# An S4 convolution beside a mixture of experts: chunks overlapped, paced by what each slot has left, and the final sums spread over the last block

## The chip, the cores and the metric

The kernel runs on one core of a Trainium2 chip. The metric is the device time of one execution in microseconds (us), as the median of several runs. A profile of one execution shows what each engine did: TensorE (PE, with its weight loads as PEld), VectorE (DVE), ScalarE (ACT), GpSimd (POOL) and SyncE (SP). Each engine takes its instructions in the order of the program and waits where a semaphore is not yet set. SP and POOL are used here to issue DMAs.

## The reference

The input is 2048 tokens of 512 channels. After a layer norm, two branches are added to the input:

```python
x = A_u
xn = _layernorm(x, axis=-1)
return x + _A_ref(xn, ...) + _B_ref(xn, ...)
```

Branch A is an S4 layer: for each of 512 channels a kernel K of length 2048 is made from 128 complex modes (`K = einsum("dn,dnl,dn->dl", Cc, P, dB).real`, with `P = exp(dt*A*l)`), the channel is convolved with it along the tokens, and `xn * Dskip` is added. Branch B is a mixture of 8 experts with top 8 of 8, so every token goes through every expert: `out += w * (silu(xn @ w1[e]) @ w2[e])` with 1792 hidden channels and softmax gates.

## The kernel before, in words

**Blocks and slots.** The experts are the main loop: 8 experts `e`, in each 4 blocks `tb` of 512 tokens, in each block 4 groups `d` of hidden channels (`DQS`: 2, 2, 2 and 1 pairs `pr` of 256), in each group 4 slots `s`. One call of `block(e, tb, d)` (L1116) issues the products with W1 (L1016, seven products in place of eight, in the manner of Strassen), and calls `slot` (L1078) after each quarter of them. Values are kept as a high and a low float16 part, and three matmuls make one product. ACT copies partial sums between PSUM banks for the next product (`hb`, L1142 and L1148), makes the activation (L1032) and its high part (L1034). DVE makes the low part (L1037). Parts of the seven products are combined by adding DMAs on POOL's queue (`add`, L1114: scC<-sE, scB<-sE). The second products, with W2 (L1000 to L1002), are taken from a list `units`, some in each slot, by `pop`. The results are scaled by the gate and added to `oacc` in DRAM by POOL's queue (L980).

**What a slot does** (L1078 to L1094), in this order: it pops units, flushes the low parts of a slot ago, runs what is pinned to this slot (`side`, filled by `put`), makes the low parts of converted weights (`work_lows`), does up to `limit` steps of weight work (`work_on`; three in the first block, two in the first and last block of an expert, else one), and lets the background go on (`bg_run`). Then the slot counter goes up. The order on each engine is the order in which Python issues the instructions, and no scheduler changes it.

**Weight work** (L376 to L510). An `Item` has a load, one to three steps, and a condition. For an expert to come, each pair of W1 and W2 is loaded once and squared on ACT (L379), which gives a scale, and later loaded again and converted. A pair of W1 takes three steps: sums of its parts on DVE into `tw` (L393 to L395), conversion of the raw parts on ACT (L382), conversion of `tw` on ACT. The low parts on DVE (L385) follow in the next slot. There is one `tw` buffer and four raw buffers. `fetch` issues loads on SP as buffers come free. Outside the first block `work_on` looks at the first item of the list alone; in the first block at the first four.

**The background** is one generator: layer norm and transposes of the tokens (`xprep`), then the S4 branch (`s4_all`, L762). It yields the planned DVE time of each piece (by `tt_(n) = n / 960 + 0.14`), or None while it waits for a slot (`hold(stamp)` waits until the slot counter is past the stamp). S4 goes in 32 chunks of 16 channels. A chunk has tables on DVE (`s4_tables`, L612 to L614, six steps), its kernel on PE (`s4_kernel`, L626, and 16 DMAs L637), its input loaded by SP (`s4_uload`, L643) and normalised on DVE (`s4_unorm`, L648, L649), transforms of input and kernel on PE (`s4_uf` L656, `s4_kf` L665), the products and sums in the transformed domain on DVE (`s4_conv`, L675 to L704), and the way back on PE (`s4_back` L713, `s4_out` L719 and a DMA to `ys4` in DRAM). Every second chunk a `s4_basis` is made for two chunks on DVE, with sines on ACT, which `run_later` lets run in slot 2 of d = 1 and d = 2 only. All PE steps of S4 share one PSUM bank; `take_bank` copies the last result out before the next is made.

In `s4_all` before, step c first normalises input c-1, then sends chunk c-2 back, transforms chunk c-1, with the tables of chunk c advanced by one step at each of these places; then the rest of the tables; then, side by side (`together`), the conv of chunk c-1, the kernel of chunk c and at times a basis.

**How much background a slot gets** (`bg_run`, L930). The planner keeps the planned PE time and the planned DVE time in `clock`. Before, the background goes on while the DVE total is under both 0.9 of the PE total and, in this slot, 1.15 of the PE time since the last slot. At the last block `bg_until("s4")` runs what is left of S4 with no other work beside it.

**The end.** `s4_final` (L1096) adds the 16 tiles of `ys4` to `oacc` by DMAs on POOL's queue (L1098) and, for the 12 tiles that are finished then, sends them to the output on SP's queue. It is pinned to one slot: expert 7, last block, d = 1, s = 0. The last four tiles are loaded again (`final_load`) and finished by DVE.

Of the kernel before, what the change touches and what calls it, by code (L numbers as in the profile page):

```python
# [13 lines left out]
ALU = mybir.AluOpType  # L14
# [3 lines left out]
P = 128  # L18
# [14 lines left out]
def s4_moe_kernel(  # L33
# [62 lines left out]

    uts = {}

    clock = {"slot": 0, "pe": 0.0, "pe0": 0.0, "dve": 0.0, "dve0": 0.0}
    bank = {"out": None}  # L100

    def take_bank(out=None):

        f, bank["out"] = bank["out"], None
        if f:
            f()
        bank["out"] = out
# [308 lines left out]

    done = set()
    work = []
    live = {"n": 0}

    def piece_square(e, w, pr, ready):
        return Item(lambda: load_raw(e, w, pr, "pp"), [lambda raw: square(e, w, pr, raw)], ready)
# [37 lines left out]
    def fetch():  # L460

        n = 0
        for it in work:
            if it.load is not None:
                if it.raw is None:
                    if live["n"] >= NRAW:
                        return
                    it.raw = it.load()
                    live["n"] += 1
                n += 1  # L470
                if n >= NRAW:
                    return

    def work_on(limit):
        while limit > 0:
            it = None
            for c in work[:4]:
                if c.ready() and not (c.sums and len(c.steps) == 3 and any(l[2] for l in lows)):
                    it = c
                    break  # L480
                if c.load is None or not early["on"]:
                    break
            if it is None:
                break
            fetch()
            if it.load is not None and it.raw is None:
                break
            low = it.steps.pop(0)(it.raw)
            limit -= 1
            last = not it.steps  # L490
            if last:
                work.remove(it)
            if low:
                lows.append((low, last, it.sums and last))
            elif last and it.load is not None:
                live["n"] -= 1
        fetch()

    early = {"on": True}

    lows = []

    def work_lows():

        while lows:
            low, last, _ = lows.pop(0)
            low()
            if last:
                live["n"] -= 1


    s4 = {}
# [75 lines left out]
    def s4_tables(c):  # L588
        g, h = c // 2, c % 2
        wv, zr, zi = s4["basis", g]  # L590
        tb = sb.tile([P, 2, 3, DC, 32], F32, tag="tb", name=f"tb{c}", bufs=1)
        V.memset(tb[:, 0, 0, :, 0:1], 1.0)
        V.memset(tb[:, 1, 0, :, 0:1], 0.0)
        V.tensor_copy(tb[:, :, 1, :, 0], wv[:, :, h * DC:(h + 1) * DC])
        for st in range(6):
            L = min(1 << st, 32)
            s0, s1, ns = (0, 2, 2) if st < 5 else (1, 2, 1)
            nn = ns * DC
            tin = tb[:, :, s0:s1, :, 0:L].rearrange("p c s d l -> p c (s d) l")
            if st < 5:  # L600
                tout = tb[:, :, 0:2, :, L:2 * L].rearrange("p c s d l -> p c (s d) l")
            else:
                tout = tb[:, :, 2, :, :]
            k0 = 2 * st
            n4 = [P, 2, nn, L]
            zrv = zr[:, h, k0:k0 + ns, :].rearrange("p k d -> p (k d)").unsqueeze(1).unsqueeze(3).to_broadcast(n4)
            ziv = zi[:, :, h, k0:k0 + ns, :].rearrange("p c k d -> p c (k d)").unsqueeze(3).to_broadcast(n4)
            ta = sb.tile([P, 1024], F32, tag="ta", name=f"ta{c}_{st}", bufs=1)[:, :2 * nn * L]
            ta = ta.rearrange("p (c n l) -> p c n l", c=2, n=nn)
            tt = sb.tile([P, 1024], F32, tag="tt", name=f"tt{c}_{st}", bufs=1)[:, :2 * nn * L]  # L610
            tt = tt.rearrange("p (c n l) -> p c n l", c=2, n=nn)
            V.tensor_tensor(ta, tin, zrv, op=ALU.mult)  # L612
            V.tensor_tensor(tt, tin[:, ::-1], ziv, op=ALU.mult)  # L613
            V.tensor_tensor(tout, ta, tt, op=ALU.add)  # L614
            yield 3 * tt_(2 * nn * L) + 0.3 * (st == 0)
        s4["tb", c] = tb

    def s4_kernel(c):
        tb = s4["tb", c]
        take_bank(lambda: s4_kernel_out(c))  # L620
        kg_ = ps_s.tile([P, 4, 64], F32, tag="s4", name=f"kgen{c}")
        for dg in range(4):
            for cc in range(2):
                for dsb in range(4):
                    d = dsb * 4 + dg
                    T.matmul(kg_[32 * dsb:32 * dsb + 32, dg, :], tb[:, cc, 0, d, :],  # L626
                             tb[:, cc, 1:3, d, :], start=(cc == 0), stop=(cc == 1))
        s4["kgen"] = kg_
        clock["pe"] += 1.2
# [94 lines left out]
    def tt_(n):  # L724

        return n / 960 + 0.14

    def hold(stamp):

        while clock["slot"] <= stamp:  # L730
            yield None

    def now():
        return clock["slot"]
# [14 lines left out]
                yield None  # L749
                waits = 0  # L750

    def s4_kgen(c, stamp):
        yield from hold(stamp + 1)
        s4_kernel(c)
        at = now()
        yield 0.0
        yield from hold(at)
        take_bank()
        s4["kt_at"] = now()
        yield 0.0  # L760

    def s4_all():  # L762
        s4_raw(0)
        for _ in s4_dt():
            yield 3.0
        yield 2.2
        yield from s4_basis(0)
        z_at = at = -1
        for c in range(NCH + 2):
            tab = s4_tables(c) if c < NCH else iter(())  # L770

            def step():
                return next(tab, 0.0)
            if 0 < c <= NCH:
                s4_unorm(c - 1)
                un_at = at = now()
                yield 2 * tt_(256) + step()
            else:
                yield step()
            yield step()  # L780
            if c > 1:
                yield from hold(z_at + 1)
                s4_back(c - 2)
                at = now()
                yield step()
                yield from hold(at)
                take_bank()
                at = now()
            else:
                yield step()  # L790
            yield step()
            if 0 < c <= NCH:
                yield from hold(max(at, un_at + 1))
                s4_uf(c - 1)
                at = now()
            yield step()
            if 0 < c <= NCH:
                yield from hold(max(at, s4["kt_at"] + 1))
                s4_kf(c - 1)
                at = now()  # L800
            yield step()
            for cost in tab:
                yield cost
            gens = []
            if 0 < c <= NCH:
                yield from hold(at)
                gens.append(s4_conv(c - 1))
            if c < NCH:
                s4_uload(c)
                gens.append(s4_kgen(c, max(at, now())))  # L810
            if c % 2 and c // 2 + 1 < NCH // 2:
                gens.append(s4_basis(c // 2 + 1))
            yield from together(gens)
            z_at = now()


    load_x(0)
# [103 lines left out]
        done.add("s4")  # L921

    bg = background()
    SHARE = 0.9

    def steps(n):
        for _ in range(n):
# [2 lines left out]
    def bg_run():  # L930


        most = clock["dve0"] + 1.15 * (clock["pe"] - clock["pe0"])
        clock["pe0"] = clock["pe"]
        while "s4" not in done and clock["dve"] < min(most, SHARE * clock["pe"]):
            c = next(bg, None)
            if c is None:
                break
            clock["dve"] += c
        clock["dve0"] = clock["dve"]  # L940

    def bg_until(key):
# [135 lines left out]
    def slot(e, tb, d, s, pops):  # L1078
        if e + tb == 0:
            work_lows()  # L1080
        pop(pops)
        flush()
        if s == 2 and 0 < d < len(DQS) - 1:
            run_later()
        for f in side.get((e, tb, d, s), ()):
            f()
        work_lows()
        early["on"] = e + tb == 0
        work_on(3 if e + tb == 0 else 2 if tb == NB - 1 or tb == 0 else 1)
        if (e, tb, d) >= (0, 2, 1):  # L1090
            if (e, tb, d, s) == (0, 2, 1, 0):
                clock["pe"] = clock["pe0"] = clock["dve"] = clock["dve0"] = 0.0
            bg_run()
        clock["slot"] += 1  # L1094

    def s4_final():  # L1096
        for i in range(NT):
            nc.gpsimd.dma_start(oacc[i], ys4[:, i, :], accum_op=ALU.add)  # L1098
            if i < NT - TPB:
                nc.sync.dma_start(out[i * P:(i + 1) * P, :], oacc[i])  # L1100
        done.add("s4f")

    put((E - 1, NB - 1, 1, 0), s4_final)

    def final_load(j):
        i = NT - TPB + j
# [139 lines left out]
```

## Time and profile before

| | us |
|---|---|
| median of 3 runs | 2522.05 (2519.59 to 2524.8) |
| the profiled execution | 2520.7 |
| its span, first to last instruction | 2518.9 |
| mean granted PE clock, share of full | 0.978 |

The profile's page gives busy time by engine and the span in slices. A table of stretches gives, for each stretch named, its length, the busy time of each engine, the granted clock and the DMA share. A row of the waits names who waited for whom, the total in us, how often, and the longest. A row of a timeline gives start, duration, engine, line, what is written and read, and in brackets how long the engine stood idle before it and what ended that. A row of the chain gives start and duration of the piece of work that the end waited for.

### The profile page before, as it was taken

The page shows a single profiled execution, that of the slowest core. Times are in us where ns is not written, and L with a number is a line of the kernel's source. Part 1 is how long each engine was busy: PE and PEld are TensorE (multiplying, and loading weights), DVE is VectorE, ACT ScalarE, POOL GpSimd, SP SyncE. Part 2 cuts the span into 40 slices and gives each one's busy share as a digit, 9 for nine tenths or more (in the row PEclk, how much of TensorE's full clock was granted, in tenths as well). Part 3 has the DMA queues.
Part 4 walks back from the last instruction along what each step waited for, and adds up shares of the span by engine and source line. Part 5 has one row for each costly group of instructions (what it writes and reads, how often), then busy time and mean ns, then how long its engine had stood idle before and what let it go on. Part 6 is the DMA issues. An engine that isn't in the chain of part 4 may idle for free.

```text
span 2518.9 us, 45497 instructions
## 1 busy us (share of the span) xinstructions
PE 2385.4 (95%) x17749; PEld 1599.0 (63%) x17749; DVE 1935.2 (77%) x3808; ACT 1418.1 (56%) x2394; POOL 346.0 (14%) x402
## 2 busy tenths in 40 slices
PE   5799889998999999999999999999999999899996
PEld 5466556655666666666666666666666666566663
DVE  7534897778879889959999879978998778986411
ACT  5666365553655647455564556665475565554442
POOL 0000001111111110111110111111011111011130
PEclk8899999999999999999999999999999999999998
DMA  7566346755656535555454554654465554434354
GB/s 233 151 159 161 75 114 150 167 110 126 140 130 139 136 75 145 110 125 127 89 151 111 131 112 98 164 130 100 109 141 117 126 136 89 126 55 78 71 124 115
DMA packets 266903, 311.32 MB, mean 124 GB/s; under 512 B 130176, under 2 KB 158848, under 8 KB 266368
## 3 DMA queue, kind: packets, MB, share of 16 engines
q1 hardware_dynamic: 209664, 212.97, 27.9%
q0 software_dynamic: 57024, 95.45, 24.2%
q8 instruction: 139, 2.28, 0.4%
q14 instruction: 76, 0.62, 0.1%
HBM read 196.11 MB, written 56.62 MB: 100 GB/s over the span
## 4 chain that ended last, share of the span: by engine, by line
PE 69%; DVE 13%; issue 7%; DMA 5%; ACT 4%; SPq 2%; POOL 1%; DVEq 0%; POOLq 0%; ACTq 0%
PE hb L1016 31%; PE y L1002 11%; PE y L1000 11%; PE y L1001 11%; DVE ahl L1037 2%; SPq L637 2%; DVE tm L695 2%; DVE w1s L385 2%; DVE s L696 1%; PE kgen L626 1%; DMA oacc<-ys 1%; PE yp L713 1%; PE uf L656 1%; PE kf L665 1%; DMA ut<-in_u_dram 1%
## 5 line engine op out<-in xcount | busy, mean ns | idle before, releaser
L1016 PE MATMUL hb<-xop,w1s 128*128 128x256 f16 x9408 | 1129.2, 276 | 80.1 <-ACT hb L1148 36.0
L1016 PEld LDWEIGHTS <-w1s 128*128 128x128 f16 x9408 | 927.0, 99 | 280.7 <-issue 75.8
L1002 PE MATMUL y<-w2s,ahl 128*128 128x512 f16 x1792 | 680.6, 380 | 8.9 <-DVE ahl L1037 8.9
L1000 PE MATMUL y<-w2s,ahl 128*128 128x512 f16 x1792 | 681.6, 380 | 0.9 <-ACT xs L256 0.8
L1001 PE MATMUL y<-w2s,ahl 128*128 128x512 f16 x1792 | 681.3, 380 | 0.0
L1002 PEld LDWEIGHTS <-ahl 128*128 128x128 f16 x1792 | 175.8, 98 | 223.6 <-DVE ahl L1037 11.4
L1114 POOL DMA_DIRECT2D scC<-sE x128 | 110.7, 865 | 1503.6 <-ACT sE L1139 1247.7
L1032 ACT ACTIVATE fa<-hb,sc 128x512 f32<-128x512 f32 (+1 forms) x256 | 162.9, 636 | 216.7 <-PE hb L1016 212.2
L696 DVE TENSOR_TENSOR s<-s,tm 128x720 f32<-128x720 f32 (+14 forms) x480 | 268.8, 560 | 16.6
L1001 PEld LDWEIGHTS <-ahl 128*128 128x128 f16 x1792 | 175.9, 98 | 166.4 <-issue 2.5
L1000 PEld LDWEIGHTS <-ahl 128*128 128x128 f16 x1792 | 176.0, 98 | 165.0 <-issue 1.9
L695 DVE TENSOR_TENSOR tm<-v,k 128x720 f32<-128x720 f32 (+14 forms) x480 | 268.0, 558 | 12.1
L1037 DVE SCALAR_TENSOR_TENSOR ahl<-fa,sc,ahl 128x512 f16<-128x512 f32 (+1 forms) x256 | 173.8, 679 | 125.4 <-ACT ahl L1034 125.1
L1037 DVE SCALAR_TENSOR_TENSOR ahl<-scB,sc,ahl 128x512 f16<-128x512 f32 (+1 forms) x128 | 87.1, 681 | 165.4 <-ACT ahl L1034 165.3
L1148 ACT COPY hb<-hb 128x512 f32<-128x512 f32 (+1 forms) x128 | 67.0, 524 | 215.8 <-PE hb L1016 215.7
L1142 ACT COPY hb<-hb 128x512 f32<-128x512 f32 (+1 forms) x128 | 66.5, 519 | 214.0 <-PE hb L1016 213.2
L1114 POOL DMA_DIRECT2D scB<-sE x128 | 111.7, 873 | 515.7 <-ACT scB L1139 286.2
L1034 ACT ACTIVATE ahl<-fa,sc 128x512 f16<-128x512 f32 (+1 forms) x256 | 171.1, 668 | 8.4
L1037 DVE SCALAR_TENSOR_TENSOR ahl<-scC,sc,ahl 128x512 f16<-128x512 f32 (+1 forms) x128 | 87.0, 680 | 112.5 <-ACT ahl L1034 112.4
L614 DVE TENSOR_TENSOR tb<-ta,tt 128x64 f32<-128x64 f32 (+2 forms) x192 | 132.2, 689 | 6.6
L612 DVE TENSOR_TENSOR ta<-tb,zr 128x64 f32<-128x64 f32 (+2 forms) x192 | 131.1, 683 | 2.5
L613 DVE TENSOR_TENSOR tt<-tb,zi 128x64 f32<-128x64 f32 (+2 forms) x192 | 130.4, 679 | 0.0
(200 smaller groups left out, 2329.9 us busy)
## 6 DMA issues: line engine op xcount, KB each, us to landing
xop<-xd SPq DMA_DIRECT2D x217, 256.0 KB, 3.4
pp<-in_w_dram SPq DMA_DIRECT2D x98, 512.0 KB, 4.5
raw<-in_w_dram SPq DMA_DIRECT2D x56, 512.0 KB, 3.9
oacc<-ye POOLq DMA_DIRECT2D x108, 256.0 KB, 6.7
scC<-sE POOLq DMA_DIRECT2D x96, 256.0 KB, 3.6
scB<-sE POOLq DMA_DIRECT2D x96, 256.0 KB, 3.4
raw<-in_w_dram SPq DMA_DIRECT2D x56, 256.0 KB, 4.0
raw<-in_w_dram SPq DMA_DIRECT2D x112, 128.0 KB, 4.1
```

The costliest lines, as they stand in the source:

```text
L612: V.tensor_tensor(ta, tin, zrv, op=ALU.mult)
L614: V.tensor_tensor(tout, ta, tt, op=ALU.add)
L695: V.tensor_tensor(tm, v3f[:, :, 0:n], kb, op=ALU.mult)
L696: V.tensor_tensor(s3[:, :, m:], s3[:, :, m:], tm, op=ALU.add)
L1000: T.matmul(y, lhs[0], w2s[pr][:, 0, fh, :], start=(c == 0), stop=False)
L1001: T.matmul(y, lhs[0], w2s[pr][:, 1, fh, :], start=False, stop=False)
L1002: T.matmul(y, lhs[1], w2s[pr][:, 0, fh, :], start=False, stop=(c == NF - 1))
L1016: T.matmul(dst[:, q, :], w1s[pr][:, a, wo, k * P:(k + 1) * P], xop[:, xo, b, k, :], start=(first_mm and q == 0 and n == 0), stop=(n == 5), ...
L1032: S.activation(fa, src[:, :n], AF.Silu, scale=sc[:, 2:3])
L1034: S.activation(ahl[:, 0, :n], fa, AF.Copy, scale=sc[:, 3:4])
L1037: V.scalar_tensor_tensor(ahl[:, 1, :n], fa, sc[:, 3:4], ahl[:, 0, :n], op0=ALU.mult, op1=ALU.subtract)
L1114: nc.gpsimd.dma_start(dst, src, accum_op=ALU.add)
```

## The change

It has three parts. Names in the diff are those above.

- `work_on` looks at the first four items in all blocks, takes only items whose load has been issued, and at most one W1 pair at a time has its sums made and not yet wholly converted (`live["tw"]`). The conversion of `tw` comes at least one slot after the sums (`now() > it.at`).
- `s4_all` runs three generators beside each other for each chunk: `s4_dve` (tables and load of chunk c+1, then conv of chunk c), `s4_pe` (transform of kernel c, way back of c-1, normalised input, kernel and transform of input of c+1) and at times the basis for later chunks. `bg_run` gives S4 in each slot what DVE's other work leaves of 0.95 of the planned PE time; what is overdrawn is carried on, and what is unused is kept up to one slot's worth.
- `s4_final` takes one tile, and the 16 tiles are pinned to the twelve slots of d = 0, 1 and 2 of the last block.

```diff
+    def can(it):
+        if not it.ready():
+            return False
+        if it.sums and len(it.steps) == 3:
+            return not live["tw"]
+        if it.sums and len(it.steps) == 1:
+            return now() > it.at
+        return True
+
     def work_on(limit):
         while limit > 0:
+            fetch()
             it = None
             for c in work[:4]:
-                if c.ready() and not (c.sums and len(c.steps) == 3 and any(l[2] for l in lows)):
+                if c.load is None:
+                    if c is work[0] and can(c):
+                        it = c
+                    break
+                if c.raw is not None and can(c):
                     it = c
-                    break
-                if c.load is None or not early["on"]:
                     break
             if it is None:
                 break
-            fetch()
-            if it.load is not None and it.raw is None:
-                break
+            if it.sums and len(it.steps) == 3:
+                live["tw"], it.at = True, now()
...
+    def s4_pe(c, st):
+        if c >= 0:
+            yield from hold(st["z"] + 1)
+            s4_kf(c)
+            st["kf"] = at = now()
+            yield 0.0
+        if c > 0:
+            yield from hold(at)
+            s4_back(c - 1)
+            at = now()
+            yield 0.0
+            yield from hold(at)
+            take_bank()
+            at = now()
+            yield 0.0
+        if c + 1 < NCH:
+            while "tab" not in st:
+                yield None
+            s4_unorm(c + 1)
+            un = now()
+            yield 2 * tt_(256)
+            yield from hold(st["tab"] + 1)
+            s4_kernel(c + 1)
+            at = now()
+            yield 0.0
+            yield from hold(at)
+            take_bank()
+            at = now()
+            yield 0.0
+            while c >= 0 and "v3" not in st:
+                yield None
+            yield from hold(max(at, un + 1, st.get("v3", -1) + 1))
+            s4_uf(c + 1)
+            yield 0.0
+
+    def s4_dve(c, st):
+        if c + 1 < NCH:
+            yield from s4_tables(c + 1)
+            s4_uload(c + 1)
+        st["tab"] = now()
+        if c >= 0:
+            while "kf" not in st:
+                yield None
+            yield from hold(st["kf"])
+            for n, cost in enumerate(s4_conv(c)):
+                if n == 0:
+                    st["v3"] = now()
+                yield cost
...
+        z = -1
+        for c in range(-1, NCH):
+            st = {"z": z}
+            gens = [s4_dve(c, st), s4_pe(c, st)]
+            if c % 2 == 0 and c + 2 < NCH:
+                gens.append(s4_next(c // 2 + 1, st))
             yield from together(gens)
-            z_at = now()
+            z = now()
...
-    SHARE = 0.9
+    SHARE = 0.95
...
-        most = clock["dve0"] + 1.15 * (clock["pe"] - clock["pe0"])
+        own = SHARE * (clock["pe"] - clock["pe0"])
         clock["pe0"] = clock["pe"]
-        while "s4" not in done and clock["dve"] < min(most, SHARE * clock["pe"]):
+        clock["left"] = min(clock["left"] + own - (clock["dve"] - clock["dve0"]), own)
+        while "s4" not in done and clock["left"] > 0:
             c = next(bg, None)
             if c is None:
                 break
-            clock["dve"] += c
+            clock["left"] -= c
         clock["dve0"] = clock["dve"]
...
-    def s4_final():
-        for i in range(NT):
-            nc.gpsimd.dma_start(oacc[i], ys4[:, i, :], accum_op=ALU.add)
-            if i < NT - TPB:
-                nc.sync.dma_start(out[i * P:(i + 1) * P, :], oacc[i])
-        done.add("s4f")
-
-    put((E - 1, NB - 1, 1, 0), s4_final)
+    def s4_final(i):
+        nc.gpsimd.dma_start(oacc[i], ys4[:, i, :], accum_op=ALU.add)
+        if i < NT - TPB:
+            nc.sync.dma_start(out[i * P:(i + 1) * P, :], oacc[i])
+
+    for i in range(NT):
+        put((E - 1, NB - 1, i * 3 // 16, i * 3 // 4 % 4), lambda i=i: s4_final(i))
```

More of the change, by code (lines that the diff above doesn't have):

```diff
@@ L97, in s4_moe_kernel @@
     uts = {}
-    clock = {"slot": 0, "pe": 0.0, "pe0": 0.0, "dve": 0.0, "dve0": 0.0}
+    clock = {"slot": 0, "pe": 0.0, "pe0": 0.0, "dve": 0.0, "dve0": 0.0, "left": 0.0}
     bank = {"out": None}
@@ L418, in s4_moe_kernel @@
     work = []
-    live = {"n": 0}
+    live = {"n": 0, "tw": False}
     def piece_square(e, w, pr, ready):
@@ L497, in work_on @@
         fetch()
-    early = {"on": True}
     lows = []
@@ L505, in work_lows @@
         while lows:
-            low, last, _ = lows.pop(0)
+            low, last, sums = lows.pop(0)
             low()
@@ L509, in work_lows @@
                 live["n"] -= 1
+            if sums:
+                live["tw"] = False
     s4 = {}
@@ L750, in together, with s4_next @@
                 waits = 0
[L752 to L760, printed above, removed]
+    def s4_pe(c, st):
[45 more added lines that the diff above has]
+                yield cost
+    def s4_next(g, st):
+        while "tab" not in st:
+            yield None
+        yield from s4_basis(g)
     def s4_all():
@@ L767, in s4_all @@
         yield from s4_basis(0)
[L768 to L812, printed above, removed]
-            yield from together(gens)
-            z_at = now()
+        z = -1
[4 more added lines that the diff above has]
+                gens.append(s4_next(c // 2 + 1, st))
+            yield from together(gens)
+            z = now()
+        yield from hold(z + 1)
+        s4_back(NCH - 1)
+        yield 0.0
+        yield from hold(now())
+        take_bank()
+        yield 0.0
     load_x(0)
@@ L1087, in slot @@
         work_lows()
-        early["on"] = e + tb == 0
         work_on(3 if e + tb == 0 else 2 if tb == NB - 1 or tb == 0 else 1)
```

## The prediction

> **What bounds the kernel now.** I read the page's busy times first, then a table of stretches, then the waits, then the chain at the end.
>
> ```profile
> PE 2385.4 (95%) x17749; PEld 1599.0 (63%) x17749; DVE 1935.2 (77%) x3808; ACT 1418.1 (56%) x2394; POOL 346.0 (14%) x402
> ```
>
> PE is busy for 95% of the span and DVE for 77%. So time can only be won where PE stands still or runs at half clock. The stretches say where that is (length, PE busy, PEld, DVE, ACT, POOL busy, granted clock, DMA share, GB/s):
>
> ```profile
> 283.00:380.00 97.00, 82.37 (x644) 53.66 (x643) 87.43 (x170) 49.55 (x80) 7.76 (x9) 0.90 0.37 99
> ...
> 500.00:630.00 130.00, 117.47 (x860) 77.32 (x859) 107.13 (x226) 59.79 (x111) 20.55 (x23) 0.93 0.54 115
> 630.00:2100.00 1470.00, 1449.66 (x10949) 973.38 (x10948) 1246.02 (x2394) 869.45 (x1484) 211.09 (x242) 1.00 0.53 123
> 2100.00:2195.00 95.00, 82.80 (x639) 54.35 (x637) 91.97 (x163) 53.15 (x86) 12.15 (x14) 0.95 0.43 101
> ...
> 2352.00:2406.00 54.00, 54.00 (x370) 36.33 (x369) 10.10 (x17) 26.37 (x44) 8.76 (x10) 1.00 0.38 67
> 2406.00:2519.00 113.00, 87.84 (x549) 54.75 (x546) 15.41 (x25) 36.49 (x65) 25.64 (x30) 0.89 0.55 121
> ```
>
> Between 283 and 2406 us, while S4 runs, PE stands still for 14.6 + 12.5 + 20.3 + 12.2 = 59.6 us (length less busy). Half clock costs about (1 - clock) x busy on top: 8.2 + 8.2 + 4.1, and I put 3 on the long stretch, whose 1.00 is rounded: 23.5. That is 83 us. The stretches that lose most are those where DVE is fullest (87.4 of 97, 92.0 of 95). In the last stretch DVE is nearly idle, and its loss has another cause. What PE waited for, in all:
>
> ```profile
> PE hb L1016 <- ACT hb L1148: 36.0, 8, 20.9
> PE hb L1016 <- ACT scC L1139: 17.8, 9, 6.0
> PE tp L247 <- ACT xh L224: 15.8, 3, 15.3
> PE hb L1016 <- ACT hb L1142: 15.0, 5, 8.9
> PE y L1002 <- DVE ahl L1037: 8.9, 4, 4.2
> PE hb L1016 <- DMA xop<-xd: 8.8, 4, 4.2
> PE yp L713 <- DVE st_w L154: 7.5, 1, 7.5
> PE kgen L626 <- DVE tb L614: 7.3, 1, 7.3
> ```
>
> The columns are total, times, longest. Apart from the start (15.3) and xop (8.8), these waits are for DVE itself or for ACT copies, which are themselves often held up behind a DVE result:
>
> ```profile
> 2177.95 0.68 DVE L393 TENSOR_TENSOR tw<-raw 128x512 f32<-128x512 f32 x1
> ...
> 2179.59 1.15 ACT L382 ACTIVATE w1s<-tw,sc 128x1024 f16<-128x1024 f32 x1 [7.08 <-DVE tw L395]
> ```
>
> ACT stood for 7.08 us at the W1 conversion, because DVE was behind with the sums. The hb copy that PE needed was queued behind it on ACT. So DVE's lateness, not its total work, is what costs PE time in the S4 phase. In the whole run after 211 us ACT waited for these sums:
>
> ```profile
> ACT w1s L382 <- DVE tw L395: 75.5, 26, 7.1
> ```
>
> The hb copies of L1142 come four to a block, one for each d, so they count blocks and slots:
>
> ```profile
> 283.00:2406.00 2123.00, 58.16 (x112) 0.99 0.51 118
> 283.00:2352.00 2069.00, 56.67 (x109) 0.99 0.52 119
> ```
>
> From 283 us, where S4's chunks begin, to the last block are 28 blocks (112 copies) of 75.8 us, or 448 slots of 4.7 us.
>
> **The change, part by part.**
>
> (1) *Final sums spread.* Now all sixteen oacc<-ys adds go onto POOL's queue at once, in the last block at d=1, slot 0:
>
> ```profile
> 2435.63 8.24 DMA oacc<-ys
> ...
> 2444.16 15.80 DMA oacc<-ys
> ...
> 2460.53 15.90 DMA scC<-sE
> ...
> 2478.46 5.28 PE hb L1016 x24
> ...
> 2486.72 2.62 PE hb L1016 x24
> ```
>
> ```profile
> scC<-sE POOLq DMA_DIRECT2D x4, 256.0 KB, 3.3
> ```
>
> The scC add queued behind them lands 15.90 us after its issue instead of 3.3, ACT cannot activate it, and PE stands for 20.9 us (the longest wait above). The 24 matmuls after it take 5.28 us against 2.62, the half clock. Together 23.6 us. Sixteen adds took 2435.6 to 2460.5, 1.6 us each. Spread over twelve slots of 4.7 us, one or two (1.6 to 3.1 us) precede each scC add, which then lands in 5 to 6.5 us. It is needed a slot and a product later, about 6 us, so the wait mostly goes. I leave 1.6 us for a late one and take **-22**. The out writes on SP's queue wait for each add, but no load that PE needs follows them in the last block. Bounds: 0, if one add in front were enough to delay it, and -23.6.
>
> (2) *A budget by slot.* The planner lets S4 spend, in each slot, what is left of 0.95 of PE's planned time after DVE's other work, and carries an overdraft on. Before, a slot could spend up to 1.15 of it, plus the overrun of the last piece (pieces are up to 3.6 us, three instructions of 1.2), which was forgiven, under an overall cap of 0.9. DVE's bursts end, and with them lateness of the kind of 7.08 us. Of the 83 us, 8.8 and some 2 of clock belong to xop, which this leaves alone. Of the other 72 I take half: **-36**. Bounds: 0 and -72. Half, because W1 sums, ahl parts and S4 pieces still share one in-order queue, and waits such as the 7.3 for tb are single events of one plan, which a new plan may repeat elsewhere.
>
> (3) *Overlapped chunks.* Conv of chunk c now runs beside tables and PE steps of c+1. The number of instructions, matmuls and DMAs stays the same. What is new is an order: the load of uc (L643) is issued at the end of the tables, and the two instructions that normalise it (L648, L649) follow on DVE after only three instructions of conv (1.2 us at the planner's price). In the trace the load comes late:
>
> ```profile
> L643 SPq DMA_DIRECT2D uc<-in_us_dram x32: 377/431/3187, 283.8 to 2272.3; - x32
> ...
> DMA to landing us min/median/max: 2.6/4.0/6.7
> ```
>
> ```profile
> 1962.16 1.23 DVE L614 TENSOR_TENSOR tb<-ta,tt 128x1024 f32<-128x1024 f32 x1
> ```
>
> ```profile
> 1960.12 13.90 SPq L370 DMA_DIRECT2D pp<-in_w_dram  x3
> 1974.07 0.42 SPq L643 DMA_DIRECT2D uc<-in_us_dram  x1
> ```
>
> Here the tables ended at 1963.4. SP was held at loads of pp, each waiting for ACT's square of a buffer, and issued uc at 1974.07. It lands about 4 us later, 15 us after the tables. Today that is hidden, since a whole conv lies between. With the new order DVE would stand between 4.0 - 1.2 = 2.8 us (SP free) and some 14 us (this case), 32 times: 90 us of DVE at the low end. Queued behind it on DVE are the rest of conv, the ahl parts that PE's second product needs, and the W1 parts. The ahl part is popped at least a slot (4.7 us) after it is queued, so the typical 2.8 is absorbed. Only the long ones reach PE: I take four of 2 us, **+8**. Bounds: 0, and +45 if half of those 90 us went through to PE.
>
> (4) *Sums converted a slot later, and the look-ahead of four in all blocks.* With a limit of two steps a slot the sums and their conversion already fell into different slots (the 7.08 us above is such a case). The new rule bites only in the first block, where the limit is three:
>
> ```profile
> ACT w1s L382 <- DVE tw L395: 2.0, 2, 1.2
> ```
>
> This is the stretch 28 to 211 us: 2.0 us of ACT in all. But the first block then does a W1 item in two slots instead of one, and ACT has less to do before each hb copy. I take **-2**, bounds +6 (a part late for its product) and -8 (the 8.9 us wait there gone). The look-ahead moves W2 conversions by a slot or two. They lie beside PE work, and I count 0.
>
> A rule that speaks against evening out DVE's load is weighed here against the trace. The POOL issue of the scC add, with DVE nearly idle (2352 to 2406) and in the S4 phase (1200 to 1400; the long stretch above has DVE busy for 1246 of 1470):
>
> ```profile
> L1114 POOL DMA_DIRECT2D scC<-sE x3 | 2.6, 867 | 33.0 <-ACT sE L1139 33.0
> ```
>
> ```profile
> L1114 POOL DMA_DIRECT2D scC<-sE x11 | 9.5, 863 | 117.0 <-ACT sE L1139 83.4 <-DVE w1s L385 14.3 <-ACT ksb L633 13.3
> ```
>
> The Trainium skill (SBUF — State Buffer, on DVE blocking DMAs that GpSimd issues) says that a DVE instruction holding the shared port pair stops GpSimd from writing descriptors. By that rule a DVE that is busy more evenly would hold up more of these adds. The row gives 863 ns against 867, so here I charge nothing.
>
> **Sum.** 2520.7 (the profiled execution, span 2518.9 and 1.8 around it) - 22 - 36 + 8 - 2 = 2468.7. That execution lies 1.35 under the median of the runs, so I forecast 2470 us.
>
> **Does S4 still end in time?** If it does not, the rest runs before the last block with PE idle. In the planner's own prices (n/960 + 0.14 us) a chunk costs 33.0 us and half a basis 5.3. The rows bear the prices out:
>
> ```profile
> L696 DVE TENSOR_TENSOR s<-s,tm 128x720 f32<-128x720 f32 (+14 forms) x480 | 268.8, 560 | 16.6
> ...
> L614 DVE TENSOR_TENSOR tb<-ta,tt 128x64 f32<-128x64 f32 (+2 forms) x192 | 132.2, 689 | 6.6
> ```
>
> Planned they are 540 and 662 ns. A block plans 68.25 us of PE and 19.4 us of other DVE work. The allowance is thus 0.95 x 68.25 - 19.4 = 45.4 us a block, before 0.9 x 68.25 - 19.4 = 42.0. The chunks add 3.78 us of PE each.
>
> ```profile
> L612 DVE TENSOR_TENSOR ta<-tb,zr x192: 258/554/1226, 284.8 to 2272.8; 128x1024 f32<-128x1024 f32 x64, 128x64 f32<-128x64 f32 x32, 128x128 f32<-128x128 f32 x32, 128x256 f32<-128x256 f32 x32
> ```
>
> ```profile
> L704 DVE TENSOR_TENSOR z<-s x32: 414/418/421, 362.5 to 2352.4; 128x256 f32<-128x256 f32 x32
> ```
>
> S4 ran from 284.8 to 2352.4. Of the 28 blocks it used some 27.2 (109 copies). Before, 32 chunks (1213 us with 15 bases) and 36 us of base and gate work, less 109 for the chunks' own PE time, over 42.0 give 27.2: the model holds. Now (1250 - 115) / 45.4 = 25.0 blocks, plus slots in which S4 can only wait, since an unused allowance is kept for one slot only. The sines of a basis run in slot 2 of d=1 and d=2 alone, and the longest way between them is twelve slots. By the allowances (some 4 us a slot up to d=2, under 2 in d=3) a basis that just misses them leaves 7 to 19 us unused, and most leave none. That is 3.9 us on average, 58 in all. With some 28 at the first and last chunks and the waits for kf, 86 us are lost, 1.9 blocks, and the last steps take a quarter. S4 then ends after 27.15 blocks, with 0.85 to spare.
>
> **Rivals.**
> *Only the end is won.* The wait for uc keeps DVE late in place of the bursts, and PE's stalls stay: 2522 - 22 plus 0 to 15 of new waits, so 2500 to 2515. For it: the 13.90 us on SP. Against it: DVE's lateness also makes uc land earlier relative to DVE, so the wait limits itself.
> *S4 does not end in time (slower).* If the waits lose over 86 + 0.85 x 45.4 = 125 us, S4 runs on before the last block. At 170 us, twice the estimate, it is 1.0 block over: 45 us of DVE work with PE idle, and about 25 of steps that wait for each other. 2470 + 70 = 2540. For it: unused allowance lapses now. Against it: 0.85 of a block.
> *All of DVE's lateness goes.* 2522 - 23.6 - 66 = 2432.
> *Descriptors held up.* If each of the 256 adds behind an evenly busy DVE took 0.1 us more of PE, 2470 + 25 = 2495. By the skill's port rule named above; the trace's 863 against 867 ns speaks against it.
>
> **How the numbers follow.** Forecast 0.57 (2445 to 2495), only the end 0.20, S4 late 0.13, all gone 0.07, descriptors 0.03. The range 2436 to 2513 leaves out S4 late and the tails, about 0.19. A measurement of this kernel tells about 0.2%, 5 us, from no change. Slower by more is S4 late, 0.13. Within it, the top of "only the end", 0.04. Faster, 0.83.
>
> **What would show it.** (1) In the last block no oacc<-ys landing over 8 us, and no PE wait over 3 us. (2) ACT's wait for tw (75.5 us in 26 waits after 211 us, up to 7.1) at less than half, and 283 to 380 and 2100 to 2195 at a clock over 0.97. (3) DVE waits for DMA uc at L648: some tens of us in all, none before. S4's last z (L704) at most a block before the last block begins. It is wrong if PE waits long before the last block with DVE busy, if L648 waits over 6 us often, or if the stalls near 360, 600 and 2170 only move.

## The result, and the profile after

The changed kernel takes 2451.5 us (2447.7 to 2455.3, 4 runs) against 2521.1 us before: ratio 0.972, 95% interval 0.970 to 0.974, so 70 us or 2.8% faster. The forecast was 2470 us, 51 below. The gain is larger than forecast, and it came out of terms that were off in both directions.

The page's busy times after:

```profile
PE 2372.7 (97%) x17749; PEld 1594.7 (65%) x17749; DVE 1937.2 (79%) x3808; ACT 1417.1 (58%) x2394; POOL 345.2 (14%) x402
```

Instruction counts and DVE's busy time are those of before, within 2 us. PE is busy for 97% of a shorter span. Cut at the first hb copy of a block (L1142 before, L1167 after), the execution falls into comparable stages. Before (length; PE, PEld, DVE, ACT, POOL busy; granted clock; DMA share; GB/s): the start up to block 3 of expert 0, the S4 phase up to block 2 of expert 7, and the last block:

```profile
0.00:287.60 287.60, 238.89 (x1788) 167.60 (x1789) 166.35 (x449) 176.67 (x279) 20.84 (x29) 0.94 0.60 167
287.60:2341.50 2053.90, 1994.20 (x14987) 1334.22 (x14985) 1733.49 (x3298) 1174.22 (x2000) 290.78 (x333) 0.99 0.52 120
2410.80:2518.90 108.10, 83.04 (x511) 51.11 (x509) 14.29 (x22) 34.49 (x60) 23.92 (x28) 0.89 0.54 118
```

The same three stages after:

```profile
0.00:285.20 285.20, 241.86 (x1788) 168.45 (x1789) 166.24 (x449) 176.29 (x279) 21.41 (x30) 0.95 0.60 169
285.20:2299.00 2013.80, 1981.50 (x14987) 1330.37 (x14985) 1734.31 (x3297) 1173.62 (x1999) 289.02 (x333) 0.99 0.53 122
2368.40:2452.50 84.10, 79.98 (x511) 49.71 (x509) 14.30 (x22) 34.44 (x60) 23.42 (x27) 1.00 0.72 151
```

The two profiled executions differ by 66.4 us (2520.7 and 2454.3): 2.4 at the start, 40.1 in the S4 phase, 24.0 in the last block, nothing in the block between (69.3 and 69.4 us). The 2.4 are those of these two executions alone: the start varies by more than that, as told at the weight work below. In the S4 phase PE does the same matmuls (14987) and stands still for 2013.8 - 1981.5 = 32.3 us in place of 59.7. What PE waits for after 200 us:

```profile
PE yp L725 <- DVE st_w L154: 12.2, 3, 5.3
PE uf L668 <- DVE st_w L154: 8.5, 2, 8.2
PE hb L1043 <- ACT scC L1164: 5.3, 7, 2.0
PE hb L1043 <- ACT hb L1173: 2.9, 2, 1.9
...
PE hb L1043 <- DMA xop<-xd: 0.5, 1, 0.5
```

The 20.9 us wait of the last block is gone. The waits for ACT copies and ahl parts are small. Most of what is left is a wait for DVE's copy of a weight total (`st_w`, L154) out of the PSUM bank that S4 shares. ACT's wait for the sums, and a DVE wait that did not exist before:

```profile
DVE uc L660 <- DMA uc<-in_us_dram: 58.7, 11, 11.6
...
ACT w1s L382 <- DVE tw L395: 15.5, 9, 3.8
```

ACT's wait fell from 77.5 us to 15.5. DVE now stands 58.7 us for the load of uc. S4's last z comes at 2312.7 us, 56 us before the first copy of the last block:

```profile
L716 DVE TENSOR_TENSOR z<-s x32: 414/418/423, 406.2 to 2312.7; 128x256 f32<-128x256 f32 x32
```

### The profile page after: what moved, and what is told of

It is laid out like the page before. It is cut to its first block, busy times and chain, and to the rows that moved or that the text cites. A ratio compares the mean times of both kernels' runs of the same rounds, so it can differ in the third digit from the quotient of the medians.

```text
span 2452.5 us, 45546 instructions
## 1 busy us (share of the span) xinstructions
PE 2372.7 (97%) x17749; PEld 1594.7 (65%) x17749; DVE 1937.2 (79%) x3808; ACT 1417.1 (58%) x2394; POOL 345.2 (14%) x402
## 4 chain that ended last, share of the span: by engine, by line
PE 59%; issue 22%; DVE 9%; POOL 3%; ACT 3%; DMA 3%; SPq 1%; POOLq 0%; DVEq 0%; ACTq 0%
PE hb L1043 26%; PE y L1027 10%; PE y L1029 10%; PE y L1028 10%; DVE ahl L1064 1%; DVE tm L707 1%; POOL scC L1139 1%; POOL scB L1139 1%; POOL oacc L1007 1%; PE yp L725 1%; DVE s L708 1%; PE kf L677 1%; PE kgen L638 1%; DMA uc<-in_us_dram 1%; DVE ta L624 1%
## 5 line engine op out<-in xcount | busy, mean ns | idle before, releaser
L1173 ACT COPY hb<-hb 128x512 f32<-128x512 f32 (+1 forms) x128 | 67.0, 523 | 211.0 <-PE hb L1043 211.0
L1167 ACT COPY hb<-hb 128x512 f32<-128x512 f32 (+1 forms) x128 | 66.5, 519 | 203.9 <-PE hb L1043 202.3
```

## The experiments

Theory after the result: the budget by slot ends DVE's lateness and with it PE's stalls in the S4 phase; overlapping the chunks makes that budget affordable; late uc gives part of it back. Rival: the overlap and the look-ahead do it, and the budget is beside the point. Ratios are to the kernel before, which ran beside each of them at medians of 2520.3 to 2520.9 us, with 95% intervals. Differences to the changed kernel are taken from its 2451.5 us.

**One part alone: the final sums.**

```diff
-    put((E - 1, NB - 1, 1, 0), s4_final)
+    for i in range(NT):
+        put((E - 1, NB - 1, i * 3 // 16, i * 3 // 4 % 4), lambda i=i: s4_final(i))
```

> The kernel before with one edit: the sixteen final S4 sums pinned to twelve slots of the last block. Theory of the prediction: the 20.9 us wait behind sixteen adds and its half clock go, -22 us, so about 2499 (ratio 0.991). Rival, that one or two adds in front of each scC add are enough to hold it up: -5 to -10 us, ratio 0.996 to 0.998.

Measured 2498.1 us, ratio 0.991 (0.990 to 0.992): -23 us. The theory holds to a microsecond, and in the profile the last block takes 84.2 us in place of 108.1.

**One part alone: the weight work** (`can`, `work_on` and `work_lows` of the diff, on the kernel before).

> The kernel before with the weight work of the change alone (look-ahead of four in all blocks, conversion of the sums a slot later, one tw in use). Theory of the prediction: it bites in the first block only, -2 us, at most -8 (ratio 0.997 to 0.999). Rival: the look-ahead is what takes ACT's 75.5 us of waits for tw away, and with them the stalls at the change of experts: -20 to -30 us, ratio 0.988 to 0.992.

Measured 2511.4 us, ratio 0.9966 (0.9954 to 0.9979): -9 us, more than my -2 and far less than the rival's. ACT's wait for tw stays at 77.3 us, and the stage table puts the gain where I had put it, at the start: block 3 of the first expert begins at 278.9 us, before at 287.6, and the S4 phase is as long as before (2053.7 us).

**Taken out of the changed kernel: the slot's delay, and the look-ahead.** Two kernels:

```diff
         if it.sums and len(it.steps) == 1:
-            return now() > it.at
+            return True
```

> The changed kernel without the rule that tw is converted a slot after the sums. Theory: the rule acts in the first block alone, where three steps go into a slot, and is what the weight part gained: +6 to +9 us, about 2459, ratio 0.975 to 0.976, all of it before 215 us. Rival, that the gain in the first block comes from the way items are chosen: within 2 us of the changed kernel, ratio 0.972.

```diff
-            for c in work[:4]:
+            for c in work[:4 if now() < 16 else 1]:
```

> The changed kernel with the look-ahead of four in the first block alone, as before; elsewhere the first item of the list. Theory of the prediction: the look-ahead there is worth nothing, within 3 us of the changed kernel, ratio 0.971 to 0.9735. Rival: it spreads the conversions at the change of experts, +5 to +15 us, ratio 0.974 to 0.978.

Without the delay 2458.4 us, ratio 0.9756 (0.9741 to 0.9771): 7 us of the gain are lost again. Without the look-ahead 2449.5 us, ratio 0.972 (0.9704 to 0.9735): no difference. So the delay is the part of the weight work that counts; the rule of one `tw` in use was not tried alone. PE's longest waits between 28 and 211 us, without the delay and with it:

```profile
PE hb L1043 <- ACT hb L1167: 10.0, 2, 9.1
PE hb L1043 <- ACT scC L1164: 7.4, 3, 5.9
PE hb L1043 <- ACT hb L1173: 5.0, 3, 2.5
```

```profile
PE hb L1043 <- ACT hb L1173: 5.7, 3, 2.9
PE hb L1043 <- ACT hb L1167: 5.3, 2, 4.5
PE y L1027 <- ACT w2s L382: 3.7, 1, 3.7
```

The long wait of 9.1 becomes 4.5, that of 5.9 becomes 0.5, and a new one of 3.7 for a W2 conversion appears. Less conversion stands on ACT ahead of the hb copies. These are the rows of ACT just ahead of the hb copy that ends the longest wait, without the delay and with it:

```profile
68.47 0.93 ACT L382 ACTIVATE w1s<-raw,sc 128x768 f16<-128x768 f32 x1
70.97 1.15 ACT L382 ACTIVATE w1s<-tw,sc 128x1024 f16<-128x1024 f32 x1 [1.56 <-DVE tw L395]
72.02 0.58 ACT L1167 COPY hb<-hb 128x512 f32<-128x512 f32 x1
```

```profile
66.33 1.14 ACT L382 ACTIVATE w1s<-tw,sc 128x1024 f16<-128x1024 f32 x1
67.38 0.57 ACT L1167 COPY hb<-hb 128x512 f32<-128x512 f32 x1
```

That all of the 7 us lie before 215 us, these two executions do not show: block 2 of the first expert begins at 214.4 us without the delay and at 213.5 with it. But among the nine kernels of this document with the delay, block 3 begins at 277.6 to 285.2 us, and the profiled execution of the changed kernel is the latest of them. In the five kernels without the delay it begins at 286.0 to 291.1 us. The means are 7.5 us apart.

**One part alone: the overlapped chunks** (`s4_pe`, `s4_dve`, `s4_next` and the new `s4_all`, with the old budget).

> The kernel before with S4's chunks overlapped and the old budget of a slot (0.9 in all, 1.15 in a slot). Theory of the prediction: the bursts stay and the wait for uc comes, so 0 to +10 us (ratio 1.000 to 1.004), with ACT's wait for tw still over 60 us. Rival: the order of the chunk, not the budget, made DVE late (after a long wait it caught up in bursts, and the overlapped chunk has no such waits): -25 to -40 us, ratio 0.984 to 0.990, and ACT's wait for tw under 30 us.

Measured 2510.9 us, ratio 0.9961 (0.9948 to 0.9973): -10 us. Both expectations missed. ACT's wait for tw is 56.4 us, so the lateness stays, as the theory says, but the new order already relieves it a little, and DVE's 63.3 us of waits for uc did not make it slower in all. The S4 phase holds nearly all of the 10 us: it takes 2044.5 us in place of 2053.9, with PE standing still for 56.6 us in place of 59.7 and busy for 1987.9 in place of 1994.2. Which waits they came from I did not separate.

**One part alone: the budget** (0.95, overdraft carried, unused allowance kept for one slot), with the old order of S4.

> The kernel before with the new budget of a slot alone (0.95, overdraft carried, unused kept for one slot) and the old order of S4. Theory of the prediction: DVE's bursts end, ACT's wait for tw is under 30 us and the stalls before the last block go, -36 us; but the old order waits for slots several times a chunk, and what is unused there lapses, so S4 does not end before the last block and the rest runs with PE idle: by more than 50 us, so slower in all (ratio 1.01 to 1.06). Rival that the waits cost little: S4 ends in time, ratio 0.985.

Measured 2597.7 us, ratio 1.030 (1.0285 to 1.0317). Both halves of the theory show in the stages, the S4 phase up to block 2 of expert 7 and that block itself:

```profile
291.10:2257.10 1966.00, 1956.48 (x14671) 1311.79 (x14670) 1571.91 (x2980) 1162.71 (x1975) 289.74 (x333) 1.00 0.54 124
2257.10:2491.80 234.70, 105.54 (x784) 69.43 (x783) 185.70 (x359) 44.78 (x82) 10.46 (x12) 0.66 0.17 33
```

In the first stretch PE stands still for 9.5 us in 1966, at full clock. ACT's wait for tw is 10.4 us. But S4 is far from done: DVE has 1572 us behind it there in place of 1733, and the rest runs ahead of the last block with PE busy for 105.5 of 234.7 us. With less DVE work in that stretch, the few stalls alone do not prove the budget. The next kernel, with about the same work in the stretch as the changed one, tests it better.

**All but the budget** (the changed kernel with the old `bg_run` and share).

> The changed kernel with the old budget of a slot put back (0.9 in all, 1.15 in a slot), all else as changed. Theory: the budget takes the lateness of DVE away and only the overlapped chunks make it affordable, so without it the three other parts add up as they did alone (-23, -9, -10): about 2480, ratio 0.984, with ACT's wait for tw over 45 us. Rival, that overlap and look-ahead together do the work: within 8 us of the changed kernel, ratio under 0.976.

Measured 2480.9 us, ratio 0.9844 (0.983 to 0.9857), as the theory says. ACT's wait for tw is back at 52.7 us, and PE stands for 55.9 us of the S4 phase:

```profile
281.50:2325.70 2044.20, 1988.29 (x14991) 1331.26 (x14990) 1745.76 (x3322) 1175.06 (x2001) 289.51 (x333) 0.99 0.52 120
```

So the budget is worth 29 us in the changed kernel, and cost 77 where the chunks were not overlapped. The rival falls. The budget differs from the old one in three things: the limit of a slot, the carried overdraft, and the cap on the total. They were not tried one by one.

**A share of 1.0.**

```diff
-    SHARE = 0.95
+    SHARE = 1.0
```

> The changed kernel with a share of 1.0 in place of 0.95. S4 ends some 1.4 blocks earlier. Theory (lateness of DVE is what the budget sets): DVE has no spare time in the S4 phase, ACT's wait for tw and PE's waits for DVE come back, +5 to +15 us, ratio 0.974 to 0.978. Rival (what counts is that an overdraft is carried on, whatever the share): within 3 us of the changed kernel, ratio 0.971 to 0.9735.

Measured 2462.5 us, ratio 0.977 (0.9757 to 0.9784): +11 us. ACT's wait for tw is 51.3 us again, and PE's waits for ACT's scC and hb (L1173) copies rise from 5.3 and 2.9 us to 10.2 and 9.9. So the carried overdraft alone does not keep DVE on time; the 5% of spare time is needed too.

**The load of uc earlier.**

```diff
-            yield from s4_tables(c + 1)
             s4_uload(c + 1)
+            yield from s4_tables(c + 1)
```

> The changed kernel with the load of uc issued ahead of the tables of the same chunk in place of behind them. DVE's waits for this DMA (58.7 us, 11 times, up to 11.6) go. Theory of the prediction: the long ones reach PE, so -8 us, about 2443, ratio 0.969. Rival: DVE's spare time takes them all in, 0 to -2 us, ratio 0.972.

Measured 2423.1 us, ratio 0.9611 (0.9598 to 0.9624): -28 us against the changed kernel. Both expectations were too low. The S4 phase:

```profile
282.10:2268.30 1986.20, 1974.71 (x14987) 1325.32 (x14986) 1734.65 (x3297) 1173.42 (x2000) 289.30 (x333) 1.00 0.53 123
```

PE stands still for 11.5 us, DVE no longer waits for uc at all, and PE's waits for `st_w` are all but gone (1.5 us at uf, 0.8 at yp), although nothing was done to that copy. How late uc is in the changed kernel shows on DVE and on SP:

```profile
1930.13 0.43 DVE L689 TENSOR_TENSOR v<-v 128x256 f32<-128x256 f32 x1
1942.11 0.43 DVE L660 TENSOR_TENSOR uc<-uc,mean 128x256 f32<-128x256 f32 x1 [11.55 <-DMA uc<-in_us_dram]
```

```profile
1927.92 7.84 SPq L370 DMA_DIRECT2D pp<-in_w_dram  x2
1935.85 0.58 SPq L732 DMA_DIRECT2D ys<-ysb  x1
1936.48 2.64 SPq L655 DMA_DIRECT2D uc<-in_us_dram  x1
```

SP is held at two pp loads until 1935.8, then issues uc; DVE stands from 1930.6 to 1942.1.

**The bank emptied by ACT.**

```diff
-        take_bank(lambda: V.tensor_copy(st, tot[:, :n]))
+        take_bank(lambda: S.copy(st, tot[:, :n]))
```

> The changed kernel with the totals of the weight squares copied out of the shared bank by ACT in place of DVE. PE's waits for that copy (12.2 us at yp, 8.2 at uf, and half clock behind them) are nearly all that is left of its stalls in the S4 phase. Theory: they go, -20 to -26 us, about 2428, ratio 0.963. Rival: the wait is for the bank and moves to ACT, which is behind as well: -5 us or less, ratio 0.970.

Measured 2427.0 us, ratio 0.9628 (0.9615 to 0.9641): -24 us, as the theory says. DVE still waits 59.4 us for uc in this kernel:

```profile
DVE uc L660 <- DMA uc<-in_us_dram: 59.4, 11, 11.5
```

So, with the new budget, a late DVE costs PE little in other ways, and much through this one copy.

**Both.**

> The changed kernel with both edits: uc loaded ahead of the tables, and the totals copied out of the bank by ACT. Alone they gave -28 and -24 us against the changed kernel. Theory: they are two places in one chain (late uc makes DVE late, DVE's copy out of the shared bank is late, PE waits), so together they give no more than the first: 2418 to 2424, ratio 0.959 to 0.9615. Rival, two separate costs that add up: about 2400, ratio 0.952.

Measured 2420.5 us, ratio 0.9607 (0.959 to 0.9625): no more than with the earlier load alone. The two are one chain: late uc, late DVE, late copy out of the bank, waiting PE. The trace of the changed kernel shows it at its longest:

```profile
549.50 0.43 DVE L660 TENSOR_TENSOR uc<-uc,mean 128x256 f32<-128x256 f32 x1 [7.23 <-DMA uc<-in_us_dram]
...
569.23 0.15 DVE L154 COPY st_w<-tot_w 128x1 f32<-128x1 f32 x1
569.43 2.08 PE L668 MATMUL uf<-uc,dftt 128*128 128x256 f32 x4 [8.22 <-DVE st_w L154]
```

DVE stands for uc until 549.5, works without a pause up to the copy at 569.2, and PE stands for 8.2 us until it is made. PE's three other waits of more than 2 us for this copy (4.0, 2.9 and 5.3 us) each come 38 us after a wait for uc, with DVE working without a pause in between. Seven of the eleven waits for uc are followed by no such wait. Both kernels beat the changed one; the earlier load needs one line moved.

**A share of 0.92: S4 brought to its limit.**

```diff
-    SHARE = 0.95
+    SHARE = 0.92
```

> The changed kernel with a share of 0.92 in place of 0.95: the rival of the prediction in which S4 does not end in time, brought about. By the prediction's sum S4 takes (1250 - 111) / 43.4 + 1.9 + 0.25 = 28.4 blocks of 28, so some 20 us of DVE work with PE idle and the steps that wait for each other: +25 to +50 us, 2475 to 2500, ratio 0.982 to 0.992. Rival: the waits shrink with the allowance, S4 ends just in time, and with less lateness: 0 to -5 us, ratio 0.970 to 0.972.

Measured 2448.7 us, ratio 0.9714 (0.9697 to 0.9731): the same as changed. In time the rival was right. In mechanism each was right by half: S4 does not end in time, as the sum said, and DVE is late less, as the rival said (ACT's wait for tw falls from 15.5 to 5.9 us):

```profile
277.60:2269.00 1991.40, 1969.95 (x14835) 1322.77 (x14834) 1686.37 (x3200) 1171.92 (x1992) 290.12 (x333) 1.00 0.53 123
2269.00:2362.40 93.40, 79.69 (x620) 53.28 (x619) 73.12 (x139) 36.17 (x66) 10.49 (x12) 0.92 0.36 68
```

S4 does not end in time. The block before the last takes 93.4 us in place of 69.4, PE standing for 13.7 of them. But the S4 phase before it is 22 us shorter than in the changed kernel, with 21.5 us of stalls in place of 32.3 and 48 us of DVE's work less in it. The two cancel.

## Why the prediction was right, and which terms were not

**The end (-22).** Right: -23 alone, -24 in the stages. Of the signs I named, no PE wait is left in the last block. But the adds did not stay under 8 us. Their median time to landing is 7.6 us, and six of the sixteen took longer than 8, the longest 14.6:

```profile
oacc<-ys POOLq DMA_DIRECT2D x16, 256.0 KB, 7.6
```

I had put an add at 1.6 us from the times of issue; in the trace of before, the last of the sixteen lands 38.8 us after the first is issued, which is 2.4 us each. The scC adds of the last block now land after 2.7 to 8.3 us, where I had put 5 to 6.5. PE felt none of it.

**The budget (-36, half of 72).** Right mechanism, size off: I halved it because single waits might come back elsewhere. Taken out of the changed kernel, the budget is worth 29 us, less than the term, but there late uc still takes part of it back. With the load of uc moved, the S4 phase falls from 2053.9 to 1986.2 us, 67.7 of the 72 that I had set as the bound. The budget and the overlap together therefore remove nearly all of DVE's lateness as PE feels it. To the overlap I gave no gain of its own; alone it gave 10 us.

**Late uc (+8).** That DVE would wait was read rightly from the trace of before. Its size was less than I had put at the low end (58.7 us against 90, eleven chunks in place of 32), and its price more: 28 us in place of 8. I had taken four waits of 2 us that reach PE; four did, but of 2.9 to 8.2 us, 20.5 in all, with half clock behind them. What I named as queued behind the waiting instruction were ahl parts and W1 parts. I left out the copy of a weight total out of the bank that S4's PE steps share, although its 7.5 us wait stood in my own list. When S4 wants the bank while that copy is still in DVE's queue, PE waits at once, with no slot of slack. The experiment with the bank emptied by ACT isolates it: 24 of the 28 us go with that copy, though the waits for uc stay. The difference between that kernel and the one with both edits, 6.5 us and hardly more than the spread of the runs, is near what I had charged for the rest.

**The first block (-2, bounds +6 and -8).** The place was right, the size not: -7 to -9. The term was read from ACT's 2.0 us of waits for tw, where the work on ACT ahead of the hb copies counted, which I had named and not priced. The look-ahead elsewhere is worth nothing, as said.

**S4's end.** The sum gave 0.85 of a block to spare; it is 56 us, three quarters. (Its check on the kernel before, 1140 over 42.0, is 27.1 blocks and not 27.2; nothing hangs on it.) At 0.92 the sum gave 0.4 of a block too much, and S4 does run over. The price of 25 to 50 us that I had set for that kernel was too high: the block before the last took 24 us more, and the S4 phase gave them back. At its worst, the budget without the overlap, S4 running over made the kernel 3% slower.

**The other signs.** In 283 to 380 and 2100 to 2195 us the clock is 1.00, before 0.90 and 0.95, and PE stands still for about 1 us in each. The stalls near 360 and 2170 are gone. That near 600 was a wait of 7.5 us for the copy `st_w`, and it is back at 569 us, 8.2 us long and for the same copy. By my own sign for being wrong, this stall only moved. It belongs to the term of uc: with uc loaded earlier it is 1.2 us long. DVE waits for uc over 6 us four times.

**The rivals.** That only the end is won is out: the S4 phase gave 40 us. A DVE that holds up POOL's descriptors would have shown in the issue of the scC adds, and does not, with DVE fuller than before (79% of the span in place of 77). Before and after:

```profile
L1114 POOL DMA_DIRECT2D scC<-sE x128 | 110.7, 865 | 1503.6 <-ACT sE L1139 1247.7
L1139 POOL DMA_DIRECT2D scC<-sE x128 | 110.5, 864 | 1487.5 <-ACT sE L1164 1236.1
```

The mean is 864 ns in place of 865. All of DVE's lateness gone, forecast at 2432 with a chance of 0.07, is what the kernel with the earlier load reaches: 2423.

The S4 terms were forecast at -36 + 8 = -28 and came at -68 + 28 = -40. Both were too small, by factors of about two and more than three, and on opposite sides. That they cancelled in part, and left the total 19 us off, is luck. A total that comes near is no proof of its terms.

## What to carry to other kernels

Pace background work by what is left in each slot, with some time to spare, but only when that work always has something to do: an allowance that lapses while it waits has to be found again at the end. When two steps are moved together, list every instruction queued behind the new wait on its engine, and ask of each whether the bound engine has slack before it. The copy of 0.15 us that frees the shared bank had none here. Issue a load as early as its buffer allows, not where its user is planned: here its place behind two other loads on SP's queue decided when it started.

## What was not expected of the hardware

Moving one load ahead of the tables took the granted clock in the S4 phase from 0.99 to 1.00 and 28 us off the time, of which only about 21 us are PE's stalls (32.3 less 11.5). The other 7 lie in PE's busy time, 1981.5 against 1974.7 us for the same 14987 matmuls: the half clock after stalls. Four matmuls of one form, after no stall and after one of 5.3 us in the changed kernel, show it:

```profile
1968.44 1.03 PE L677 MATMUL kf<-kt,dftt 128*128 128x256 f32 x4
1980.07 2.08 PE L725 MATMUL yp<-z,dftt 128*128 128x256 f32 x4 [5.28 <-DVE st_w L154]
```

The size fits what the prediction had charged, 23.5 us of half clock for 59.6 us of stalls: from before to the kernel with the earlier load, the stalls of the S4 phase fall by 48.2 us and PE's busy time by 19.5. Not expected was that so much of both hung on one load.
